# Two blocks of linear attention on one core: KV products in pairs of 64-column tiles, with a new order behind them

## The chip, the cores and the metric

The kernel runs on one core of one Trainium2 chip. The metric is the device time of one execution in microseconds (us); lower is better. The time before is the median of three runs. The profile is one execution, taken by the hardware profiler; its times count from the first instruction of the program.

The engines have these names in the profile: PE is TensorE (matrix products), PEld its weight loads, DVE is VectorE, ACT is ScalarE, POOL is GpSimd, SP is SyncE, which here only issues DMAs. A product has a stationary operand, which PEld loads, and a moving one, which streams through the array; the result lands in PSUM, and DVE or ACT bring it back into SBUF.

## The reference

Two blocks of linear attention, A and B, read the same x (2048 x 640) with weights of their own; a gate per row mixes their outputs. There are 32 heads of Dh = 20 columns.

```python
def block(x, wqkv, wo):
    q, k, v = heads(x @ wqkv)                 # 32 heads of 20
    phi = lambda t: where(t > 0, t + 1, exp(t)) + 1e-6
    pq, pk = phi(q), phi(k)
    kv = einsum("bhsd,bhse->bhde", pk, v)     # 20 x 20 for each head
    z = pk summed over s
    o = (pq @ kv) / (pq . z + 1e-6)
    return o @ wo                             # heads side by side
g = sigmoid((x * gate_w).sum(-1))
out = g * block(A_x, A_wqkv, A_wo) + (1 - g) * block(A_x, B_wqkv, B_wo)
```

## The kernel before

S = 2048 rows are 16 tiles of P = 128, D = 640 columns are DT = 5 chunks of 128, and HF = 320 is half of D. For each block b the kernel goes through these steps:

- `k_chunk` (L225, products L216) makes phi(k) of 128 rows into pk, and `q_unit` (L274, products L280) makes phi(q), turned, into pqT[b].
- `g_all` (L692) makes G = x^T phi(k), 640 x 640, in GT: two halves `lo, hi = GT` of 320 columns, with five chunks of 128 rows each. Chunk 4 comes from `g_pass` (L306); the other four come from one level of Strassen's scheme in `g_strassen` (L374, products L369), which computes seven products of sums. The sums are DVE's work. In between stands `rec_pass` (L509): the denominators, whose products den (L175) have 32 weight columns and 256 moving columns and run in four column tiles of the array; then reciprocals, a DMA through DRAM (`r_store`, `r_load`) that spreads them, and `scale` (L569), which multiplies pqT by them on DVE. `p_diff` (L543) is a DVE difference of two parts of pqT[0].
- `kv_mm` (L450, products L455) makes wv^T G, so the rows are those of v and the columns those of k. Only the 20 x 20 blocks on the diagonal are wanted. It therefore takes groups of columns of widths WB = (120, 120, 80) in each half: NW = 6 groups of six, six and four heads. For each group five products over the chunks accumulate in PSUM. `kv_mask` (L460) multiplies the groups by maskE, a pattern of ones in 20 x 20 blocks, on DVE and puts them into KVA: two operations for each half.
- `m_mm` (L483) multiplies each group of KVA by its rows of wo, two products of 320 columns. The result M = kv wo goes to DRAM (`m_store`, L489) and comes back in another layout (`m_load`, L493).
- At the end, the output pq_A M_A + pq_B M_B, with the gate in pq, is again made by Strassen's scheme: class `Pair` (L593, products in `prod`, L579) has products p1 to p7 for the two row tiles i and i + 8, five accumulating products of 320 columns each. `p1` and `p5` are copied out of PSUM by ACT. `p_sums` (L548) and `m_sum` (L559) are the sums that they need, on DVE: p5 of pair i needs p_sums(.., (1,)) of its 128 rows, and TM[0], which is m_sum(0).

The order of instructions on each engine is that of the program text around the change (`tc.manual_schedule`, L723); the preparation at the start, on POOL among others, is ordered by a scheduler.

In stage A the KV products are in `kv_a` (L470), between k_chunk(1, 1) and k_chunk(1, 2); `m_a(k)` (L498), one group at a time, stands between later chunks, from k_chunk(1, 4) on.

In stage B (L754 to L810) they stand where the output products begin. The eight PSUM banks are oz0, oz1, ox0, ox1 (for p1 and p5) and s0 to s3. The order is: KV products of the first half into s2, its mask, pairs[0].p1, a scale, KV products of the second half into s3, its mask, m_sum(0), m_b(0), pairs[1].p1, m_b(1), m_b(2), pairs[2].p1, p_sums, m_b(3), m_b(4), p_sums, pairs[3].p1, m_b(5), the two loads of M_B, pairs[0].p5, p_sums. `m_b(k)` (L767) is two products (L485), into s0 and s1 for even k and s2 and s3 for odd k, two copies, and a store; both copies of m_b(0) are ACT's, and of the others the first is ACT's and the second DVE's.

wo is loaded by `load_wo` (L665), four DMAs, so that the rows of a group lie on partitions 0 to w. In stage A this stands after the load of wv; in stage B inside g_strassen (L422).

Of the kernel before, what the change touches and what calls it, by code (L numbers as in the profile page):

```python
# [8 lines left out]
P = 128  # L9
FP32 = mybir.dt.float32  # L10
BF16 = mybir.dt.bfloat16
ACT = mybir.ActivationFunctionType
ALU = mybir.AluOpType

S, D, H = 2048, 640, 32
Dh = D // H
DT = D // P
# [4 lines left out]
HF = D // 2  # L22
TW = 4
WB = (120, 120, 80)
NW = 6
EPS = 1e-6
RB = 256
SH = S // 2
# [3 lines left out]
def kernel(  # L32
# [11 lines left out]
    nc = tc.nc  # L44
# [32 lines left out]
    wo_sb = [None, None]  # L77
    ident = persist.tile([P, P], BF16, name="ident")
    headE = persist.tile([P, H], BF16, name="headE")
    maskE = persist.tile([P, WB[0]], BF16, name="maskE")  # L80
    KVA = persist.tile([P, NW, WB[0]], BF16, name="KVA")
    R = [persist.tile([P, 4 * RB], BF16, name=f"R{h}") for h in range(2)]
    ones = persist.tile([P, H], BF16, name="ones")
# [55 lines left out]


    make_identity(nc, ident[:])
    nc.gpsimd.memset(maskE[:], 1.0)
    for sign, base in ((1, 0), (-1, Dh - 1)):
        nc.gpsimd.affine_select(
            out=maskE[:], in_=maskE[:], pattern=[[-sign * Dh, WB[0] // Dh], [0, Dh]],
            compare_op=ALU.is_ge, fill=0.0, base=base, channel_multiplier=sign,
        )
    nc.gpsimd.memset(headE[:], 1.0)
    for sign, base in ((1, 0), (-1, TW - 1)):
        nc.gpsimd.affine_select(  # L150
# [223 lines left out]
    def g_strassen(b, den):  # L374

        x11, x12 = [xn[:, k:k + hc, 0:ic] for k in (0, hc)]
        x22 = xn[:, hc:ST, ic:2 * ic]
        b11 = pk[:, 0:hc, 0:HF]
        b21, b22 = [pk[:, hc:ST, n * HF:(n + 1) * HF] for n in range(2)]
        lo, hi = GT  # L380

        def temp(name):
            return work.tile([P, 2, HF], FP32, tag="osb", name=name, bufs=3)

        def add(dst, pt, sb):
            nc.vector.tensor_tensor(out=dst, in0=pt[:, :, 0:HF], in1=sb[:], op=ALU.add)

        even, odd = ps("gs0", 0), ps("gs1", 1)
        g_prod(even, x11, b11, True, 0, 1 - b)
        rec = den()  # L390
        rec(0)
        g_prod(even, x11, b11, True, 1 - b)
        p1 = temp("p1")
        nc.scalar.copy(out=p1[:], in_=even[:, :, 0:HF])
        if b == 0:
            x_sum(3)
        else:
            rec(1)
        g_prod(odd, SX[2], TK[b][2], True)
        u2 = temp("u2")  # L400
        add(u2[:], odd, p1)
        if b == 0:
            x_sum(4)
        else:
            p_diff(part[2])
            p_diff(part[3])
        g_prod(even, x12, b21, False)
        nc.scalar.copy(out=lo[:, 0:2, :], in_=even[:, :, 0:HF])
        if b == 0:
            rec(1)  # L410
        r_load(b, 1, nc.scalar)
        if b == 0:
            wq[1] = load_w(1, "q", nc.scalar)
        scale(b, 0, 2, 0)
        g_prod(odd, SX[3], TK[b][3], False)
        u3 = temp("u3")
        add(u3[:], odd, p1)
        scale(b, 2, 4, 0)
        even = ps("gs0", 0)
        g_prod(even, SX[1], TK[b][1], True)  # L420
        if b == 1:
            load_wo(1, nc.sync)  # L422
        add(hi[:, 2:4, :], even, u3)
        scale(*((b, 0, 2, 1) if b else (b, 4, 5, 0)))
        g_prod(odd, x22, TK[b][4], False)
        if b == 1:
            scale(1, 4, 5, 0)
        add(lo[:, 2:4, :], odd, p1)
        if b == 1:
            scale(1, 2, 4, 1)  # L430
        g_prod(even, SX[4], b22, False)
        for n in range(2):
            nc.vector.tensor_tensor(out=hi[:, n, :], in0=even[:, n, 0:HF], in1=u2[:, n], op=ALU.add)
        if b == 0:
            scale(0, 0, 2, 1)
# [11 lines left out]
        )  # L447
        return zsel

    def kv_mm(b, dst, hf):  # L450

        for i, w in enumerate(WB):
            d0 = i * WB[0]
            for c in range(DT):
                nc.tensor.matmul(  # L455
                    dst[:w, d0:d0 + w], lhsT=wv[b][:, c, hf * HF + d0:hf * HF + d0 + w],
                    rhs=GT[hf][:, c, d0:d0 + w], start=(c == 0), stop=(c == DT - 1),
                )

    def kv_mask(src, hf):  # L460

        for i, n in ((0, 2), (2, 1)):
            w = WB[i]
            nc.vector.tensor_tensor(
                out=KVA[:w, 3 * hf + i:3 * hf + i + n, 0:w],
                in0=src[:w, i * WB[0]:i * WB[0] + n * w].rearrange("p (i n) -> p i n", i=n),
                in1=maskE[:w, None, 0:w].to_broadcast([w, n, w]), op=ALU.mult,
            )

    def kv_a():  # L470

        pt = ps("kvA")
        for hf in range(2):
            kv_mm(0, pt[:, hf], hf)
        for hf in range(2):
            kv_mask(pt[:, hf], hf)

    def m_rows(k):
        hf, i = divmod(k, 3)
# [2 lines left out]

    def m_mm(b, k, dst, n):  # L483
        w = m_rows(k)[1]
        nc.tensor.matmul(  # L485
            dst[:w, 0:HF], lhsT=KVA[:w, k, 0:w], rhs=wo_sb[b][:w, k, n * HF:(n + 1) * HF], start=True, stop=True,
        )

    def m_store(b, k, part):  # L489
# [174 lines left out]

    def load_wo(b, eng):  # L665
        t = wo_sb[b] = wpool.tile([P, NW, D], BF16, tag="wo", name=f"wo{'AB'[b]}")
        for hf in range(2):
            for i, n in ((0, 2), (2, 1)):
                w, d0 = WB[i], hf * HF + i * WB[0]
                eng.dma_start(  # L670
                    out=t[:w, 3 * hf + i:3 * hf + i + n, :],
                    in_=wo_dram[b][d0:d0 + n * w, :].rearrange("(j p) f -> p j f", p=w),
                )

    def q_pass(b, units, sums, lifted):

# [46 lines left out]
    with tc.manual_schedule():  # L723
# [37 lines left out]
        with late_pool("mid") as mid:  # L761
            def single(k):
                return bank(mid, f"s{k}")

            first = [single(k) for k in range(4)]

            def m_b(k):  # L767
                part = pk[:, k, :].rearrange("p (b n) -> p b n", b=2)
                w = m_rows(k)[1]
                dst = [first[n] if k == 0 else single(k % 2 * 2 + n) for n in range(2)]  # L770
                for n in range(2):
                    m_mm(1, k, dst[n], n)
                for n, copy in enumerate((nc.scalar.copy, nc.vector.tensor_copy if k else nc.scalar.copy)):
                    copy(out=part[:w, n], in_=dst[n][:w, 0:HF])
                m_store(1, k, part)

            kv_mm(1, first[2], 0)
            kv_mask(first[2], 0)
            pairs[0].p1()
            scale(1, 4, 5, 1)  # L780
            kv_mm(1, first[3], 1)
            kv_mask(first[3], 1)
            m_sum(0)
            m_b(0)
            pairs[1].p1()
            m_b(1)
            m_b(2)
            pairs[2].p1()
            p_sums(slice(0, P), (1,))
            m_b(3)  # L790
            m_b(4)
            p_sums(slice(P, 2 * P), (1,))
            pairs[3].p1()
            m_b(5)
            for h in range(2):
                m_load(1, h * P // 2, (h + 1) * P // 2)
            pairs[0].p5()
            p_sums(part[1], (1,))
        pairs[1].p5()
        for n in (2, 3):  # L800
# [74 lines left out]
```

## Time and profile before

| | us |
|---|---|
| median of 3 runs | 183.33 |
| lowest and highest run | 183.22, 184.1 |
| span of the profiled execution | 181.9 |
| PE busy | 177.9 |
| DVE busy | 147.2 |
| ACT busy | 86.3 |
| KV products, stage A (chain) | 1.49 |
| KV products, stage B (chain) | 0.74 and 0.74 |

The span goes from the first to the last instruction of the profiled execution. That execution has no time of its own in the records beside its span; the median of the runs stands 1.43 us above the span. The mean granted TensorE clock is 1.000. A row of the chain is the start, the length, and what the time went to; a row of the timeline the start, the length from first start to last end, engine, line, operation, output and inputs, shapes, count, and in brackets the idle time before it with what ended it. Matmuls overlap: one of 320 columns has a duration of 299 ns, but the next starts 136 ns after it.

### The profile page before, as it was taken

Reading aid. Unit: us, or ns where it says so; the run is one execution under the profiler, and the core shown is the slowest. Engines: PE = TensorE matmul, PEld = TensorE weight load, DVE = VectorE, ACT = ScalarE, POOL = GpSimd, SP = SyncE. Lnnn points to the kernel's source line nnn. Section 1 sums busy time; section 2 is a strip of 40 time slices with the busy share of each in tenths; the row PEclk is TensorE's granted clock in tenths of the full one; section 3 lists DMA queues with packets and bytes.
Section 4 is the critical chain, followed back from the end, with each engine's and each line's share of the span. In section 5 each row is a group of like instructions: output and inputs, shape, how many; then the busy total and the mean of one; then the engine's idle time right before and its main releaser. Section 6 shows DMA issues by size and latency. Waiting matters only on the chain.

```text
span 181.9 us, 3296 instructions
## 1 busy us (share of the span) xinstructions
PE 177.9 (98%) x1285; PEld 120.7 (66%) x1285; DVE 147.2 (81%) x248; ACT 86.3 (47%) x141; POOL 2.5 (1%) x18
## 2 busy tenths in 40 slices
PE   8999999999999999999999999999999999999993
PEld 3566657765577777877775555577778777777772
DVE  0386868989998896788778999969799999877863
ACT  2245846889961101378784779921102863111010
POOL 4100000000000000000000000000000000000000
PEclk9999999999999999999999999999999999999999
DMA  5899999423100116241115000000343570133323
GB/s 177 207 248 189 224 373 310 85 52 130 58 0 8 67 45 211 77 137 37 56 34 191 17 0 0 0 0 18 126 105 84 174 188 0 40 108 108 114 90 126
DMA packets 22598, 19.17 MB, mean 105 GB/s; under 512 B 10294, under 2 KB 21814, under 8 KB 22582
## 3 DMA queue, kind: packets, MB, share of 16 engines
q1 hardware_dynamic: 20644, 16.82, 33.4%
q10 hardware_dynamic: 1938, 2.13, 3.5%
q8 instruction: 10, 0.16, 0.4%
q14 instruction: 6, 0.05, 0.1%
HBM read 12.13 MB, written 4.53 MB: 92 GB/s over the span
## 4 chain that ended last, share of the span: by engine, by line
PE 95%; DMA 2%; ACTq 0%; DVE 0%; issue 0%
PE gs L369 17%; PE kA L216 12%; PE ox L583 12%; PE kB L216 12%; PE qB L280 12%; PE qA L280 6%; PE oz L583 6%; PE qA L290 5%; PE gB L328 2%; PE gA L328 2%; PE ow L583 2%; DMA R<-in_gate_w_dram 2%; PE qA L300 1%; PE s L485 1%; PE mA L485 1%; PE kvA L455 1%
## 5 line engine op out<-in xcount | busy, mean ns | idle before, releaser
L216 PEld LDWEIGHTS <-xT 128*128 128x128 bf16 x320 | 31.1, 98 | 12.5 <-issue 0.2
L208 DVE TENSOR_SCALAR e<-e 128x640 bf16<-128x640 bf16 (+2 forms) x53 | 18.9, 357 | 8.1 <-ACT e L203 7.4
L216 PE MATMUL kB<-wkB,xT 128*128 128x320 bf16 x160 | 23.0, 299 | 0.0
L216 PE MATMUL kA<-wkA,xT 128*128 128x320 bf16 (+1 forms) x160 | 22.6, 300 | 0.2 <-DMA wkA<-in_A_wqkv_dram 0.2
L280 PE MATMUL qB<-xT,wqB 128*128 128x512 bf16 x100 | 21.7, 379 | 0.0
L203 ACT ACTIVATE e<-kB 128x640 bf16<-128x640 f32 x16 | 11.3, 704 | 16.2 <-DMA wqB<-in_B_wqkv_dram 9.4
L280 PEld LDWEIGHTS <-wqB 128*128 128x128 bf16 x100 | 11.7, 117 | 9.7
L203 ACT ACTIVATE e<-kA 128x640 bf16<-128x640 f32 x16 | 11.2, 705 | 8.5 <-PE kA L216 8.5
L203 ACT ACTIVATE e<-qA 128x1024 bf16<-128x1024 f32 (+1 forms) x11 | 10.4, 946 | 6.4 <-PE qA L290 5.1
L633 ACT COPY u<-ox 128x320 f32<-128x320 f32 x8 | 3.4, 426 | 20.4 <-PE ox L583 20.4
L203 ACT ACTIVATE e<-qB 128x1024 bf16<-128x1024 f32 x10 | 10.2, 1024 | 5.6 <-PE qB L280 4.9
L369 PEld LDWEIGHTS <-xn 128*128 128x128 bf16 x96 | 9.2, 98 | 3.9 <-issue 0.4
L369 PEld LDWEIGHTS <-S 128*128 128x128 bf16 x96 | 9.4, 98 | 3.6
L280 PE MATMUL qA<-xT,wqA 128*128 128x512 bf16 x50 | 11.0, 379 | 0.0
L212 DVE SCALAR_TENSOR_TENSOR pk<-kB,e 128x640 bf16<-128x640 f32 x12 | 9.9, 825 | 1.3
L583 PEld LDWEIGHTS <-xT 128*128 128x128 bf16 x85 | 8.1, 98 | 2.9
L583 PEld LDWEIGHTS <-pqTB 128*128 128x128 bf16 x80 | 7.8, 98 | 3.2
L583 PEld LDWEIGHTS <-pqTA 128*128 128x128 bf16 x80 | 7.7, 98 | 2.9
L369 PE MATMUL gs<-pk,xn 128*128 128x320 bf16 x64 | 9.5, 299 | 0.0
L280 PEld LDWEIGHTS <-wqA 128*128 128x128 bf16 x50 | 5.9, 117 | 4.8
L290 PE MATMUL qA<-xT,wqA 128*128 128x512 bf16 x40 | 9.0, 379 | 0.0
L210 DVE TENSOR_TENSOR pk<-pk,e 128x640 bf16<-128x640 bf16 x12 | 5.9, 493 | 2.8 <-ACT pk L207 2.1
(122 smaller groups left out, 297.7 us busy)
## 6 DMA issues: line engine op xcount, KB each, us to landing
out_dram<-pk SPq DMA_DIRECT2D x14, 160.0 KB, 1.8
xn<-in_A_x_dram SPq DMA_DIRECT2D x3, 640.0 KB, 6.3
wkB<-in_B_wqkv_dram SPq DMA_DIRECT2D x1, 800.0 KB, 4.6
wqB<-in_B_wqkv_dram ACTq DMA_DIRECT2D x1, 800.0 KB, 5.1
wvB<-in_B_wqkv_dram SPq DMA_DIRECT2D x1, 800.0 KB
MA<-mA_dram SPq DMA_DIRECT2D x1, 800.0 KB, 4.2
MB<-mB_dram SPq DMA_DIRECT2D x2, 400.0 KB, 4.5
wqA<-in_A_wqkv_dram SPq DMA_DIRECT2D x2, 320.0 KB, 4.2
```

Source lines behind the costliest of these rows:

```text
L203: nc.scalar.activation(out=e[:], in_=src, func=ACT.Exp)
L208: nc.vector.tensor_scalar(e[:], e[:], 1.0, EPS, op0=ALU.min, op1=ALU.add)
L210: nc.vector.tensor_tensor(out=dst, in0=dst, in1=e[:], op=ALU.max)
L212: nc.vector.scalar_tensor_tensor(out=dst, in0=src, scalar=1.0 + EPS, in1=e[:], op0=ALU.add, op1=ALU.max)
L216: nc.tensor.matmul(pt[:, hf, 0:w], lhsT=xT[:, c, i * P:(i + 1) * P], rhs=wk[b][:, c, hf * HF:hf * HF + w], start=(c == 0), stop=(c == DT - 1),
L280: nc.tensor.matmul(pt[:, u, :], lhsT=mixed(wq[b][:, c, :], m), rhs=xT[:, c, n * HB:(n + 1) * HB], start=(c == 0), stop=(c == DT - 1),)
L290: nc.tensor.matmul(pt[:, u, :], lhsT=mixed(wq[b][:, c, :], m + u), rhs=xT[:, c, n * HB:(n + 1) * HB], start=(c == 0), stop=(c == DT - 1),)
L328: nc.tensor.matmul(pt[:, hf, 0:HF], lhsT=xn[:, i, c * P:(c + 1) * P], rhs=pk[:, i, hf * HF:(hf + 1) * HF], start=(i == 0), stop=(i == ST - 1),
L369: nc.tensor.matmul(pt[:, n, 0:HF], lhsT=left[:, i, n * P:(n + 1) * P], rhs=right[:, i, :], start=(first and i == 0), stop=(i == hc - 1), s ...
L485: nc.tensor.matmul(dst[:w, 0:HF], lhsT=KVA[:w, k, 0:w], rhs=wo_sb[b][:w, k, n * HF:(n + 1) * HF], start=True, stop=True,)
L583: nc.tensor.matmul(dst, lhsT=left[:, c, r0:r0 + P], rhs=right[:, c, :], start=(first and c == 0), stop=(c == DT - 1), skip_group_check=not ...
L633: nc.scalar.copy(out=self.u6[:], in_=self.at("x"))
```

## The change

- WT = 60: a group of 120 becomes two of 60 (three heads each), a group of 80 becomes 60 and 20. `kv_groups(k)` gives both, the first with its output on PSUM partitions 0 to 59, the second on 64 to 123 (or 64 to 83). `kv_mm` issues them in turn with tile_position (0, 0) and (0, 64), and the chunks in the order 4, 2, 3, 0, 1. All six groups go into one bank, 60 columns each; both halves are made in one pass.
- `kv_mask` takes four operations: the first rows of all six groups, then the second rows of two, two, and the two narrow ones. There are two masks, maskE[0] and maskE[1], the second shifted for the rows from 64 on. KVA keeps its columns, with rows 60 to 63 between the two parts; it is zeroed at the start, on POOL, as the blocks off the diagonal are no longer written.
- `m_mm` contracts over 124 rows (or 84) instead of 120 (or 80), and `load_wo` puts the rows of wo to match, with six DMAs instead of four.
- In stage B pairs[0].p1 comes ahead of the KV products, and these are in one piece; m_sum(0) moves up into `g_strassen`, behind p_diff(part[3]); pairs[1].p1 and pairs[2].p1 come between the KV products and m_b(0); m_b(0) and m_b(1), and m_b(2) and m_b(3), stand together; pairs[0].p5 comes ahead of m_b(4) and m_b(5).

```diff
--- before.py
+++ after.py
@@ -23,6 +23,7 @@
 TW = 4
 WB = (120, 120, 80)
 NW = 6
+WT = 60
 EPS = 1e-6
 RB = 256
 SH = S // 2
@@ -77,7 +78,7 @@
     wo_sb = [None, None]
     ident = persist.tile([P, P], BF16, name="ident")
     headE = persist.tile([P, H], BF16, name="headE")
-    maskE = persist.tile([P, WB[0]], BF16, name="maskE")
+    maskE = [persist.tile([P, WT], BF16, name=f"maskE{r}") for r in range(2)]
     KVA = persist.tile([P, NW, WB[0]], BF16, name="KVA")
     R = [persist.tile([P, 4 * RB], BF16, name=f"R{h}") for h in range(2)]
     ones = persist.tile([P, H], BF16, name="ones")
@@ -139,12 +140,14 @@
 
 
     make_identity(nc, ident[:])
-    nc.gpsimd.memset(maskE[:], 1.0)
-    for sign, base in ((1, 0), (-1, Dh - 1)):
-        nc.gpsimd.affine_select(
-            out=maskE[:], in_=maskE[:], pattern=[[-sign * Dh, WB[0] // Dh], [0, Dh]],
-            compare_op=ALU.is_ge, fill=0.0, base=base, channel_multiplier=sign,
-        )
+    for r in range(2):
+        nc.gpsimd.memset(maskE[r][:], 1.0)
+        for sign, base in ((1, 0), (-1, Dh - 1)):
+            nc.gpsimd.affine_select(
+                out=maskE[r][:], in_=maskE[r][:], pattern=[[-sign * Dh, WT // Dh], [0, Dh]],
+                compare_op=ALU.is_ge, fill=0.0, base=base - sign * r * P // 2, channel_multiplier=sign,
+            )
+    nc.gpsimd.memset(KVA[:], 0.0)
     nc.gpsimd.memset(headE[:], 1.0)
     for sign, base in ((1, 0), (-1, TW - 1)):
         nc.gpsimd.affine_select(
@@ -404,6 +407,7 @@
         else:
             p_diff(part[2])
             p_diff(part[3])
+            m_sum(0)
         g_prod(even, x12, b21, False)
         nc.scalar.copy(out=lo[:, 0:2, :], in_=even[:, :, 0:HF])
         if b == 0:
@@ -447,33 +451,38 @@
         )
         return zsel
 
-    def kv_mm(b, dst, hf):
-
-        for i, w in enumerate(WB):
-            d0 = i * WB[0]
-            for c in range(DT):
-                nc.tensor.matmul(
-                    dst[:w, d0:d0 + w], lhsT=wv[b][:, c, hf * HF + d0:hf * HF + d0 + w],
-                    rhs=GT[hf][:, c, d0:d0 + w], start=(c == 0), stop=(c == DT - 1),
-                )
-
-    def kv_mask(src, hf):
-
-        for i, n in ((0, 2), (2, 1)):
-            w = WB[i]
+    def kv_groups(k):
+
+        hf, i = divmod(k, 3)
+        w = WB[i]
+        return [(r * P // 2, hf, i * WB[0] + r * WT, min(WT, w - r * WT)) for r in range(2)]
+
+    def kv_mm(b, dst):
+
+        for k in range(NW):
+            for i, c in enumerate((4, 2, 3, 0, 1)):
+                for p0, hf, d0, w in kv_groups(k):
+                    nc.tensor.matmul(
+                        dst[p0:p0 + w, k * WT:k * WT + w], lhsT=wv[b][:, c, hf * HF + d0:hf * HF + d0 + w],
+                        rhs=GT[hf][:, c, d0:d0 + w], start=(i == 0), stop=(i == DT - 1), tile_position=(0, p0),
+                    )
+
+    def kv_mask(src):
+
+        src = src[:, 0:NW * WT].rearrange("p (k n) -> p k n", k=NW)
+        for r, ks, w in ((0, slice(0, NW), WT), (1, slice(0, 2), WT), (1, slice(3, 5), WT), (1, slice(2, NW, 3), WB[2] - WT)):
+            rows = slice(r * P // 2, r * P // 2 + w)
+            n = len(range(NW)[ks])
             nc.vector.tensor_tensor(
-                out=KVA[:w, 3 * hf + i:3 * hf + i + n, 0:w],
-                in0=src[:w, i * WB[0]:i * WB[0] + n * w].rearrange("p (i n) -> p i n", i=n),
-                in1=maskE[:w, None, 0:w].to_broadcast([w, n, w]), op=ALU.mult,
+                out=KVA[rows, ks, r * WT:r * WT + w], in0=src[rows, ks, 0:w],
+                in1=maskE[r][rows, None, 0:w].to_broadcast([w, n, w]), op=ALU.mult,
             )
 
     def kv_a():
 
         pt = ps("kvA")
-        for hf in range(2):
-            kv_mm(0, pt[:, hf], hf)
-        for hf in range(2):
-            kv_mask(pt[:, hf], hf)
+        kv_mm(0, pt[:, 0])
+        kv_mask(pt[:, 0])
 
     def m_rows(k):
         hf, i = divmod(k, 3)
@@ -482,8 +491,9 @@
 
     def m_mm(b, k, dst, n):
         w = m_rows(k)[1]
+        rows = P // 2 - WT + w
         nc.tensor.matmul(
-            dst[:w, 0:HF], lhsT=KVA[:w, k, 0:w], rhs=wo_sb[b][:w, k, n * HF:(n + 1) * HF], start=True, stop=True,
+            dst[:w, 0:HF], lhsT=KVA[:rows, k, 0:w], rhs=wo_sb[b][:rows, k, n * HF:(n + 1) * HF], start=True, stop=True,
         )
 
     def m_store(b, k, part):
@@ -664,13 +674,15 @@
 
     def load_wo(b, eng):
         t = wo_sb[b] = wpool.tile([P, NW, D], BF16, tag="wo", name=f"wo{'AB'[b]}")
-        for hf in range(2):
-            for i, n in ((0, 2), (2, 1)):
-                w, d0 = WB[i], hf * HF + i * WB[0]
-                eng.dma_start(
-                    out=t[:w, 3 * hf + i:3 * hf + i + n, :],
-                    in_=wo_dram[b][d0:d0 + n * w, :].rearrange("(j p) f -> p j f", p=w),
-                )
+        tv = t[:].rearrange("p (h i) f -> p h i f", h=2)
+        wide = wo_dram[b].rearrange("(h r) f -> h r f", h=2)
+        for r, n in ((0, P // 2), (1, WT)):
+            r0, p0 = r * WT, r * P // 2
+            for hf in range(2):
+                src = wide[hf, 0:2 * WB[0], :].rearrange("(j p) f -> p j f", j=2)
+                eng.dma_start(out=tv[p0:p0 + n, hf, 0:2, :], in_=src[r0:r0 + n])
+            n, d0 = (n, WB[2] - WT)[r], 2 * WB[0] + r0
+            eng.dma_start(out=tv[p0:p0 + n, :, 2, :], in_=wide[:, d0:d0 + n, :].rearrange("h p f -> p h f"))
 
     def q_pass(b, units, sums, lifted):
 
@@ -774,27 +786,24 @@
                     copy(out=part[:w, n], in_=dst[n][:w, 0:HF])
                 m_store(1, k, part)
 
-            kv_mm(1, first[2], 0)
-            kv_mask(first[2], 0)
             pairs[0].p1()
             scale(1, 4, 5, 1)
-            kv_mm(1, first[3], 1)
-            kv_mask(first[3], 1)
-            m_sum(0)
+            kv_mm(1, first[2])
+            kv_mask(first[2])
+            p_sums(slice(0, P), (1,))
+            pairs[1].p1()
+            pairs[2].p1()
             m_b(0)
-            pairs[1].p1()
             m_b(1)
+            pairs[3].p1()
             m_b(2)
-            pairs[2].p1()
-            p_sums(slice(0, P), (1,))
             m_b(3)
+            p_sums(slice(P, 2 * P), (1,))
+            pairs[0].p5()
             m_b(4)
-            p_sums(slice(P, 2 * P), (1,))
-            pairs[3].p1()
             m_b(5)
             for h in range(2):
                 m_load(1, h * P // 2, (h + 1) * P // 2)
-            pairs[0].p5()
             p_sums(part[1], (1,))
         pairs[1].p5()
         for n in (2, 3):
```

## The prediction

> **What bounds the kernel now.** I read the page first (busy times, then the shares of the chain that ended last), then the chain in order of time, then single stretches of the timeline.
>
> ```profile
> span 181.9 us, 3296 instructions
> ...
> PE 177.9 (98%) x1285; PEld 120.7 (66%) x1285; DVE 147.2 (81%) x248; ACT 86.3 (47%) x141; POOL 2.5 (1%) x18
> ...
> PE 95%; DMA 2%; ACTq 0%; DVE 0%; issue 0%
> ```
>
> The chain in order of time (start, length, what):
>
> ```profile
> 70.25 2.72 PE kB L216 x20
> 72.96 1.49 PE kvA L455 x30
> ...
> 137.76 0.74 PE s L455 x15
> 138.50 0.68 PE ox L583 x5
> 139.18 0.74 PE s L455 x15
> ...
> 145.65 0.68 PE oz L583 x5
> ```
>
> The page says that TensorE is busy for 98% of the span, and that 95% of the last chain is TensorE with nothing waited for. The pieces of the chain touch each other: 138.50 + 0.68 = 139.18, and so on. So a nanosecond taken from TensorE's queue is a nanosecond of the total, and a nanosecond in which TensorE waits is one lost, because no idle time later takes it up. The KV products that the change rewrites (L455) are 1.49 us in stage A and 0.74 + 0.74 = 1.48 us in stage B: 2.97 us of 181.9, so even a large gain here is a small part. The span is 181.9 and the median of the runs 183.33; the 1.43 us between them lie outside the span, and I leave them as they are. Everything below is a difference to the span. For this kernel a measurement can tell about 0.5%, or 0.92 us, from no change.
>
> **The products themselves.** Before, a pass has 30 products, of 120x120 and 80x80. After, it has 60 (30 pairs, of 60 columns beside 60, or 60 beside 20), each pair in two column tiles that can run side by side. The trace has no pair of this size. Nearest are the old products and the den products (L175), which run four side by side in tiles of 32 columns.
>
> ```profile
> 137.65 0.38 PE L455 MATMUL s<-GT,wvB 128*120 128x120 bf16 x4
> 138.15 0.35 PE L455 MATMUL s<-GT,wvB 128*80 128x80 bf16 x5
> L455 PE MATMUL s<-GT,wvB 128*120 128x120 bf16 x20 | 1.4, 218 | 0.0
> L455 PE MATMUL s<-GT,wvB 128*80 128x80 bf16 x10 | 0.7, 204 | 0.0
> 120.94 0.30 PE L328 MATMUL gB<-pk,xn 128*128 128x320 bf16 x1
> 121.17 0.29 PE L175 MATMUL denB<-pqTB,zsel 128*32 128x256 bf16 x4
> 121.18 0.10 PEld L175 LDWEIGHTS <-zsel 128*32 128x32 bf16 x4
> L175 PEld LDWEIGHTS <-zsel 128*32 128x32 bf16 x80 | 2.0, 96 | 0.6 <-DVE zsel L444 0.3 <-issue 0.3
> 121.17 1.27 PE L175 MATMUL denB<-pqTB,zsel 128*32 128x256 bf16 x40
> 122.37 2.35 PE L369 MATMUL gs<-pk,xn 128*128 128x320 bf16 x16
> ```
>
> The step from one start to the next: four products of 120 take 0.38 in all and one takes 0.218, so the step is (0.38 - 0.218) / 3 = 54 ns. For 80: (0.35 - 0.204) / 4 = 37 ns. The line through both is 0.43 ns a column; at 60 columns it gives 28 ns, and I take 30 for one product of 60 with its weight load.
>
> Do two such products share those 30 ns? The den rows say yes for tiles of 32: four products that last about 0.27 each are over 0.29 after the first began, so they start within 0.02, and four weight loads with a mean of 96 ns are done in 0.10 together. Ten rounds of four have starts from 121.17 to 121.17 + 1.27 - 0.28 = 122.16, so a round takes 0.11, about what 256 columns cost alone at 0.43 ns. I take 30 ns a pair. The ends: 26 ns below (a line with less overhead), 60 above (nothing shared). The forecast lies at the low end because the den rows are the nearest.
>
> Going into column tiles and out of them costs something as well. A product of 320 columns has a step of 2.72 / 20 = 0.136; gB's last starts at 120.94, so the next would start at 121.08, but den starts at 121.17: 0.09. At the other side den's last round starts at 122.16, its step of 0.11 is over at 122.27, and gs starts at 122.37: 0.10. Together 0.2 us a pass, counted in full.
>
> A pass then takes 30 x 0.030 + 0.2 = 1.10 us. Stage A: 1.10 - 1.49 = -0.39. Stage B: 1.10 - 1.48 = -0.38. **Sum -0.77 us.** Break-even for the products alone is (1.485 - 0.2) / 30 = 43 ns a pair.
>
> [...]
>
> **Masks, zeros, weights of wo.** DVE has four masks a pass as before, with 640 columns in sum as before (360 + 120 + 120 + 40 against 240 + 80, twice). I cost them at nothing in stage A, where their first reader on TensorE, mA, comes behind three k_chunks, 30 products of the 0.136 us worked out above. The POOL additions stand at the start of the kernel.
>
> ```profile
> 1.00 0.20 POOL L142 MEMSET maskE<- 128x120 bf16 x1
> 1.29 0.30 POOL masks.py:199 TENSOR_SCALAR_AFFINE_SELECT ident<-ident 128x128 bf16<-128x128 bf16 x1
> 3.62 1.25 PE L240 MATMUL xt<-ident,xn 128*128 128x128 bf16 x10
> 133.44 1.76 SPq L670 DMA_DIRECT2D woB<-in_B_wo_dram  x4
> woB<-in_B_wo_dram SPq DMA_DIRECT2D x2, 100.0 KB, 4.3
> ```
>
> The zeroing of KVA (720 columns, at most 6 x 0.20 = 1.2) goes ahead of the identity, which was ready at 1.59 and is then ready by about 2.8; TensorE reads it first at 3.62. Nothing, with 0.8 to spare. wo takes six DMAs instead of four. In B they begin at 133.44 at 0.44 each, so the last is issued at about 135.7 and lands 4.3 later, at 140.0. The products that read it (m_b) come from 140.7 on (worked out below), and SP has nothing else until then. Nothing.
>
> **m_sum(0) moved ahead.** It leaves the stretch after the KV products and goes into stage B's Strassen products.
>
> ```profile
> 140.42 0.98 DVE L539 TENSOR_TENSOR TM<-MA 128x1600 bf16<-128x1600 bf16 x1
> 130.25 1.23 DVE L572 TENSOR_TENSOR pqTB<-pqTB,R 128x2048 bf16<-128x2048 bf16 x1 [0.96 <-DMA R<-rB_dram]
> 137.80 0.89 DVE L433 TENSOR_TENSOR GT<-gs,u 128x320 bf16<-128x320 f32 x2
> ```
>
> It takes 0.98, and stands just ahead of the scale that waited 0.96 for a DMA: it fills a hole. If some 0.1 spills over, the next reader with a wait is the KV product on the last GT chunk: DVE finishes that at 137.80 + 0.89 = 138.69. After the change TensorE first does pairs[0].p1 (from 137.6, 0.68), then enters the tiles (0.09), and the late chunk is the 19th pair at the earliest (18 x 0.03): about 138.9. Nothing. pairs[0].p1 waits for the same DVE add as the old first KV product.
>
> **The new order behind the KV products in B.** I count from the start of pairs[1].p1: time 0, which is 137.60 + 0.68 (pairs[0].p1) + 0.09 + 0.90 + 0.10 = 139.37 in the span. A block of five is 0.68, an m_b (two products of 320 columns) 0.272. TensorE then has p1(1) 0, p1(2) 0.68, m_b(0) 1.36, m_b(1) 1.63, p1(3) 1.91, m_b(2) 2.59, m_b(3) 2.86, p5(0) 3.14, m_b(4) 3.82, m_b(5) 4.09, p5(1) 4.37, p1(4) 5.05, p5(2) 5.73.
>
> ```profile
> 139.95 0.55 DVE L464 TENSOR_TENSOR KVA<-s,maskE 120x240 bf16<-120x240 f32 x2 [0.21 <-PE s L455]
> 139.21 0.43 ACT L612 COPY xn<-ox 128x320 f32<-128x320 f32 x1 [9.37 <-PE ox L583]
> 141.24 0.75 ACT L774 CAST pk<-s 120x320 bf16<-120x320 f32 x2
> 141.32 0.88 DVE L774 CAST pk<-s 120x320 bf16<-120x320 f32 x2
> 143.72 0.48 DVE L774 CAST pk<-s 80x320 bf16<-80x320 f32 x1
> 144.12 2.28 DVE L539 TENSOR_TENSOR pqTA<-pqTA,pqTB 128x1280 bf16<-128x1280 bf16 x3
> 151.76 1.36 PE ow L583 x10
> 144.75 2.02 SPq L494 DMA_DIRECT2D MB<-mB_dram  x2
> MB<-mB_dram SPq DMA_DIRECT2D x2, 400.0 KB, 4.5
> ```
>
> A copy starts 0.03 after the chain piece that it reads (139.18, 139.21), so about 0.3 after its product's start. On ACT it lasts 0.43, and back to back 0.32 apart (0.75 for two); on DVE 0.48, and 0.40 apart. ACT: p1(2)'s copy from 1.56 (end of its piece 1.53, plus 0.03), then m_b(0) twice at 1.88 and 2.20, then m_b(1) at 2.52, done at 2.95. m_b(3) writes the bank that this last copy reads, and wants to start at 2.86: with a wake-up it starts at 3.0. **A stall of 0.14** that before had slack, since there p1 stood after each one or two m_b. Behind it everything shifts by 0.14.
>
> DVE: two old masks took 0.55, so four take about 1.1; they follow the last KV product, and m_b(0) comes at 1.36. No stall, 0.2 to spare. The cast of m_b(4) starts at 3.82 + 0.14 + 0.14 (its second product) + 0.33 = 4.43, that of m_b(5) at 4.83, and the p_sums of rows 256 to 511 at 5.23, done 0.81 later: 6.04. The p5(2) that reads it wants to start at 5.73 + 0.14 = 5.87: **a stall of about 0.21**. Before, these sums were done at 144.12 + 0.81 = 144.93, over 0.5 before that block (the chain has it from 145.65). The cause is that p5(0) now stands ahead of m_b(4) and m_b(5), so the casts come later while p5(2) does not. The sums for p5(1) are done near 4.35 against 4.51: no stall, but close.
>
> MB: the last cast ended at 144.20 and the second load, issued at about 146.3, landed 4.5 later, at 150.8. Now the cast ends at 139.37 + 4.83 + 0.48 = 144.7, so MB lands at 151.3, against TensorE's need near 151.6 (its first product with MB starts one product's latency ahead of the piece at 151.76). Nothing, with 0.3 to spare.
>
> **Sum.** -0.77 + 0.14 + 0.21 = -0.42 us: a span of 181.5 and a time of 183.33 - 0.42 = 182.9.
>
> **The rivals.**
> *No sharing at this size.* The place is the KV pass: each small product takes its own 30 ns. For it: the forecast needs four instructions fed every 30 ns, where den needs only eight every 110. Against: den's loads and products start together. A pass is 60 x 0.03 + 0.2 = 2.0, so +0.51 and +0.52, with the stalls +0.35: +1.4, 184.7. With both stalls it loses against before from a pair of (2.97 - 0.4 - 0.35) / 60 = 37 ns on. [...]
> *The stalls do not come.* ACT and DVE are quicker at handing over than I add up; the gain stays whole: -0.77, 182.6. For it: each stall is the difference of sums with errors of 0.1. Against: both orders of copies are fixed.
> *MB comes late.* The 0.3 to spare goes, since six stores and two loads stand in a row on SP. A last store that lands 0.7 later costs 0.4: 183.3.
>
> **How the numbers follow.** Forecast 0.58 (182.9), no sharing 0.22 (184.7; a part of it, pairs between 37 and 52 ns, ends within 0.92 of before), no stalls 0.12 (182.6), MB late 0.08 (183.3). Faster by over 0.5% means below 182.4, which needs pairs of 26 ns and no stalls (-1.0): 0.06. Slower by over 0.5%, above 184.25: nearly all of no sharing, and a little of MB: 0.20. Within: 0.74. The range goes from that low end, 182.4, to no sharing, 184.7.
>
> **What would show it.** In the profile after: the kvA piece of the chain near 1.1 (2.0 if nothing is shared); starts two by two in the KV lines, as den has them by fours; an idle TensorE ahead of m_b(3) and of p5(2), released by ACT and DVE; no idle at the start. A kvA piece above 1.5 makes the forecast wrong, as does a TensorE wait of over 0.5 us in B.

## The result, and the profile after

The changed kernel takes 188.68 us (median of 6 runs, 187.82 to 189.48) against 183.42 for the kernel before (6 runs, 183.06 to 184.1): **a ratio of 1.0287, 95% interval 1.0267 to 1.0306**. The forecast was 182.9 with a range up to 184.7, so the change is slower by 5.3 us where next to nothing was forecast.

The page of the kernel after: span and instructions, busy time of the engines, the granted clock in 40 slices, the shares of the chain that ended last.

```profile
span 187.5 us, 3425 instructions
...
PE 182.8 (97%) x1340; PEld 122.6 (65%) x1345; DVE 147.6 (79%) x248; ACT 86.2 (46%) x141; POOL 3.4 (2%) x22
...
PEclk9999999999999999999999999999997899999999
...
PE 90%; DMA 6%; DVE 1%; issue 1%; SPq 0%
```

TensorE is busy for 182.8 us, 4.9 more than before: most of the loss is not waiting but products that take longer. Two slices late in the span have a granted clock below 9 tenths, and 6% of the chain is DMA. The chain of the kernel after, in order of time:

```profile
72.58 3.13 PE kvA L465 x60
75.71 4.18 PE kB L219 x30
...
139.81 3.14 PE s L465 x60
142.94 0.94 PE ox L593 x5
143.88 1.33 PE oz L593 x5
...
151.76 5.21 DMA MB<-mB_dram
157.02 1.53 PE ow L593 x10
```

A KV pass is 3.13 us where it was 1.49; the forecast had 1.10 and named a piece above 1.5 as the sign that it is wrong. The piece behind it in stage A, 30 products of 320 columns, is 4.18, and in the chain of the kernel before it is 4.07:

```profile
74.45 4.07 PE kB L216 x30
```

Leaving the column tiles costs 0.11. In stage B blocks of five, 0.68 before, take 0.94 and 1.33.

Where in the pass is the time? The same kernel, the KV line alone, in the stretches of its groups (start and end, length, PE and PEld busy with the number of instructions that touch the stretch, clock, DMA share, GB/s):

```profile
72.50:72.82 0.32, 0.31 (x20) 0.31 (x21) 1.00 0.00 0
72.82:74.07 1.25, 1.25 (x22) 0.95 (x16) 1.00 0.00 0
74.07:74.39 0.32, 0.32 (x21) 0.31 (x21) 1.00 0.00 0
74.39:75.65 1.26, 1.26 (x22) 0.95 (x15) 1.00 0.00 0
```

The first stretch holds two groups of 120 columns, ten pairs of 60 beside 60, in 0.32 us. The second holds one group of 80, five pairs of 60 beside 20, in 1.25 us: 0.25 a pair. The trace's starts say the same more finely: in the groups of 120 the two products of a pair start 3 ns apart and the pairs 30 ns apart (72.561, 72.591, 72.621); in the groups of 80 the starts alternate at 0.144 and 0.110 (73.063, 73.207, 73.317, 73.461). TensorE counts as busy all the while. The pass is 20 x 0.030 + 10 x 0.254 = 3.14 us.

The blocks of 0.94 and 1.33 are another thing. First the kernel after, then the kernel before in the same stretch of time (busy time of PE, PEld, DVE, ACT, POOL, then the clock):

```profile
142.90:143.50 0.60, 0.60 (x6) 0.45 (x6) 0.52 (x1) 0.00 (x0) 0.00 (x0) 0.95 0.00 0
143.50:146.90 3.40, 3.40 (x15) 2.20 (x14) 1.58 (x6) 1.84 (x5) 0.00 (x0) 0.51 0.01 2
146.90:147.50 0.60, 0.60 (x6) 0.52 (x5) 0.00 (x0) 0.16 (x1) 0.00 (x0) 1.00 0.41 90
```

```profile
142.90:146.90 4.00, 4.00 (x32) 2.92 (x30) 4.00 (x8) 2.78 (x8) 0.00 (x0) 1.00 0.76 237
```

For 3.4 us TensorE is granted half its clock (0.51) and a product of 320 columns has a step of 0.267 instead of 0.136; 13 steps lose 1.7 us. The timeline of the kernel after shows four m_b products in that stretch and four of the same kind after it:

```profile
145.00 1.27 PE L495 MATMUL s<-woB,KVA 124*120 124x320 bf16 x4
...
148.37 0.71 PE L495 MATMUL s<-woB,KVA 124*120 124x320 bf16 x4
```

This happens in some runs only: of the six, three have a mean granted clock of 0.991 and 189.18 to 189.48 us, three 0.999 to 1.000 and 187.82 to 188.17, so it costs 1.3 us where it comes, and the profiled run (189.25) has it.

**The account**, from the starts of the two traces. Stage A, from the den products to the last Strassen product of stage B: 83.54 before, 85.29 after, +1.75 (1.64 of KV pieces and 0.11 of leaving the tiles). From there to pairs[0].p2: 14.14 before, 18.19 after, +4.05, which are 1.66 of KV products, 0.11 of leaving the tiles, 1.68 of half clock, and TensorE waits of 0.04 (p5 of pair 1), 0.19 (p5 of pair 2) and 0.38 (MB). The products to the end +0.01, the tail behind the last product +0.25, the start -0.38. Sum 5.68; the spans are 181.86 and 187.54.

### The profile page after: what moved, and what is told of

Its sections match the earlier page's. It is cut to its first block, busy times and chain, and to the rows that moved or that the text cites. A ratio compares the mean times of both kernels' runs of the same rounds, so it can differ in the third digit from the quotient of the medians.

```text
span 187.5 us, 3425 instructions
## 1 busy us (share of the span) xinstructions
PE 182.8 (97%) x1340; PEld 122.6 (65%) x1345; DVE 147.6 (79%) x248; ACT 86.2 (46%) x141; POOL 3.4 (2%) x22
## 4 chain that ended last, share of the span: by engine, by line
PE 90%; DMA 6%; DVE 1%; issue 1%; SPq 0%
PE gs L372 16%; PE kA L219 12%; PE kB L219 12%; PE qB L283 11%; PE ox L593 10%; PE qA L283 6%; PE qA L293 5%; PE oz L593 4%; DMA MB<-mB_dram 3%; PE gA L331 2%; PE gB L331 2%; PE ow L593 2%; DMA wkA<-in_A_wqkv_dram 2%; PE s L465 2%; PE kvA L465 2%; PE qA L303 1%
```

## The experiments

**The theory**: the time goes into the changes of width, from a product of 60 columns to one of 20 (a step of about 0.14 in the trace of the kernel after) and back (0.11), where a pair of 60 takes 0.03. Groups of 80 alternate 60, 20, 60, 20 and pay this ten times, with the change on leaving the group. With one width a pass should fall from 3.13 to about 1.1, the half clock of stage B should go with it, and the time should be 182.8 to 183.4. **The rival on the pass**: 60 short instructions can't be fed fast enough, whatever their widths. **A second question**: are the steps behind the products, the stalls that the forecast saw, and MB as priced?

**All tiles of one width.** Each group is covered by two products of 60 columns that overlap in the middle, so that the number of products stays and only the width of the small ones changes. Masks, rows of M and wo follow.

```diff
     def kv_groups(k):
...
-        return [(r * P // 2, hf, i * WB[0] + r * WT, min(WT, w - r * WT)) for r in range(2)]
+        return [(r * P // 2, hf, i * WB[0] + r * (w - WT), WT) for r in range(2)]
```

> The narrow product of the two groups of 80 is made 60 columns wide (it computes columns 20 to 79 and keeps the last 20), so all 60 products of a pass are of one width; their number, the order and everything else is that of the changed kernel. [...] Rival (the feed of 120 short instructions runs dry from the 22nd product on): the number of instructions is the same, a pass stays at about 3.1 and the time at 188 to 189.

Measured: 183.65 us, 1.0013 of the kernel before (1.0003 to 1.0023). Its chain:

```profile
72.45 1.02 PE kvA L465 x60
...
137.56 1.02 PE s L465 x60
...
145.86 5.38 DMA MB<-mB_dram
```

The same 60 products, ten of them three times as wide, take 1.02 us instead of 3.13. Feeding is not the limit; the rival falls. With 0.11 for leaving the tiles the pass is 1.13, 0.36 to 0.37 under the old 1.49, and stage A's stretch shrinks by that: 83.54 to 83.17. Yet the kernel is not faster than before, and lies above the 182.8 to 183.4 that were expected. Its timeline shows why:

```profile
141.10 0.87 PE L495 MATMUL s<-woB,KVA 124*80 124x320 bf16 x4
...
142.49 0.71 PE L495 MATMUL s<-woB,KVA 124*120 124x320 bf16 x4
...
143.72 0.84 PE L593 MATMUL ox<-MA,pqTA 128*128 128x320 bf16 x5
144.64 0.85 PE L593 MATMUL oz<-TM,pqTA 128*128 128x320 bf16 x5
...
151.29 1.40 PE L593 MATMUL ow<-MB,pqTB 128*128 128x320 bf16 x9 [0.36 <-DMA MB<-mB_dram]
```

Four m_b products take 0.87 in the first row and 0.71 in the second: the 0.16 is m_b(3) waiting for its bank (it starts at 141.54; ACT's copy of m_b(1) out of that bank ends at 141.49). The last block of 0.84 before p5(2) begins at 143.72, and p5(2) at 144.64 instead of 143.72 + 0.68 = 144.40: 0.24. The first product with MB starts 0.52 later than the steps before it would have it (0.36 of that as idle PE). Together 0.93 in stage B, against 0.37 gained there: its stretch grows from 14.14 to 14.71.

**The same products in another order.** In the groups of 80 the five of 60 columns go first, then the five of 20, so each such group has two changes of width, one inside and one on leaving it, instead of ten.

```diff
-            for i, c in enumerate((4, 2, 3, 0, 1)):
-                for p0, hf, d0, w in kv_groups(k):
+            steps = [(i, c, g) for i, c in enumerate((4, 2, 3, 0, 1)) for g in kv_groups(k)]
+            if k % 3 == 2:
+                steps.sort(key=lambda s: s[2][0])
+            for i, c, (p0, hf, d0, w) in steps:
```

> The 20-wide products stay, but in the groups of 80 the five products of 60 come first and the five of 20 behind them, so there are 3 changes of width inside a pass instead of 20. Theory of the changes: a pass of 0.6 for the four groups of pairs, 0.55 for 20 single products, 0.2 for entering and leaving and 3 x 0.12 for the changes, 1.7 us; the time 183.4 + 0.4 + 0.2 to 0.7 = 184.0 to 184.5 us. Rival (a product of 20 columns is slow by itself, 0.14 us each wherever it stands): 10 x 0.14 more than the pairs alone, a pass of 2.4 to 2.6 us, and 185.5 to 187.

Measured: 185.01 us, 1.0081 (1.0068 to 1.0095). Chain:

```profile
73.01 1.55 PE kvA L467 x60
...
138.65 1.55 PE s L467 x60
```

No instruction is added or taken away, and the pass falls from 3.13 to 1.55. In the trace the 20-column products start 25 ns apart among themselves and the 60-column ones of a single tile 30; the steps over the two changes of a group are 0.12 and 0.10. The time is above the 184.0 to 184.5 that were expected: the sum allowed 0.2 to 0.7 for waits in stage B, and they are 1.00 (0.16, 0.24 and 0.60 for MB), with 0.25 more behind the last product.

**Another width of the narrow one.** Groups of 80 as 60 beside 40, which leaves the products unequal. If any change of width costs the time, the pass stays near 3.1 us and the time near 188; if only a change as large as the one from 60 to 20 does, they are 1.02 and 183.65.

```diff
-        return [(r * P // 2, hf, i * WB[0] + r * WT, min(WT, w - r * WT)) for r in range(2)]
+        n = min(WT, w // 2)
+        return [(0, hf, i * WB[0], WT), (P // 2, hf, i * WB[0] + w - n, n)]
```

> As e1_wide, but the narrow product is 40 columns wide instead of 60 (it computes columns 40 to 79 of the group and keeps the last 20); order as in the changed kernel. [...]

Measured: 183.91 us against 183.56 in that series, 1.0015 (0.9996 to 1.0034). Chain (the trace has all 60 products of a pass; where two run side by side the chain can hold one of them alone):

```profile
73.04 1.01 PE kvA L466 x54
...
138.14 1.01 PE s L466 x56
```

Unequal products cost nothing, 60 beside 40 runs like 60 beside 60 (1.01 and 1.02 in the chains). So it is not inequality: of the two widths tried beside 60, 20 costs time and 40 does not. Weight columns and moving columns were narrowed together, so the runs do not tell which of the two counts.

**Narrow in one stage only**, the other as in the first experiment (masks and wo follow):

```diff
-    def kv_groups(k):
+    def kv_groups(b, k):
...
+        if b == 0:
+            return [(r * P // 2, hf, i * WB[0] + r * WT, min(WT, w - r * WT)) for r in range(2)]
```

and the same with `b == 1`.

> The narrow products of 20 columns in stage A alone; stage B has one width of 60; order as changed. Theory of the width changes: stage A's pass 3.1 us, 2.0 more than in e1_wide, so 185.7 us. The halved clock: if a pass with 20 width changes is what brings it, it comes behind stage A's pass in some of the runs (mean clock 0.991, 1.3 us more) and never in stage B; if it belongs to stage B's order or its waits, the clock stays 1.0 here.

> The narrow products of 20 columns in stage B alone; stage A has one width of 60; order as changed. Theory of the width changes: stage B's pass 3.1 us, 2.0 more than in e1_wide, 185.7 us at a full clock, and about 187 where the clock is halved behind the pass. If the clock belongs to stage A's slow pass: no run here with 0.991.

Measured: 186.1 us for A (1.0164, 1.0133 to 1.0195), 185.84 for B (1.0137, 1.0116 to 1.0158). Chains, A then B:

```profile
73.02 3.13 PE kvA L467 x60
...
140.24 1.02 PE s L467 x60
```

```profile
73.27 1.02 PE kvA L467 x60
...
138.38 3.13 PE s L467 x60
```

The slow pass comes where the 20s are and costs 2.2 to 2.5 us over the first experiment (the median of A holds two runs with the half clock), 3.13 - 1.02 = 2.11 of it seen in the chain. On the half clock: narrow in A has it in two of six runs (0.991 and 0.989 at 187.13 and 187.63, the others 0.999 or 1.000 at 185.81 to 186.26), narrow in B in none of four. None of the other kernels' runs, about 170 with those of before, has less than 0.997. So it goes with a slow pass, also in stage A; it doesn't follow each one.

**The order alone**: the old products, with the new order behind them; the first line added is the one in g_strassen.

```diff
+            m_sum(0)
...
-            kv_mm(1, first[2], 0)
-            kv_mask(first[2], 0)
             pairs[0].p1()
             scale(1, 4, 5, 1)
-            kv_mm(1, first[3], 1)
-            kv_mask(first[3], 1)
-            m_sum(0)
+            for hf in range(2):
+                kv_mm(1, first[2 + hf], hf)
+            for hf in range(2):
+                kv_mask(first[2 + hf], hf)
...
```

> The kernel before with nothing but the new order of stage B and the earlier m_sum(0); KV products, masks and wo as before. If the stalls worked out ahead are right (m_b(3) 0.14, pairs[2].p5 0.21, and MB landing late by up to 0.4): 183.4 + 0.4 to 0.8 = 183.8 to 184.2 us. Rival (the order costs nothing by itself; the stalls in the changed kernel come from its slow KV pass): 183.4 us, within 0.1.

Measured: 183.76 us, 1.0009 (0.9987 to 1.0031). Timeline:

```profile
142.19 0.87 PE L486 MATMUL s<-woB,KVA 80*80 80x320 bf16 x4
...
144.81 0.84 PE L584 MATMUL ox<-MA,pqTA 128*128 128x320 bf16 x5
145.72 0.85 PE L584 MATMUL oz<-TM,pqTA 128*128 128x320 bf16 x5
```

The same two waits, 0.16 and 0.24 (145.72 - 144.81 - 0.68 = 0.23), and 0.12 for MB, with the old products: they belong to the order. The stretch is 0.53 longer by the trace; the runs' interval does not exclude no change.

**The products alone**: pairs of 60 with the old order (two passes of three groups in B, m_b and p1 interleaved as before); against the first experiment's kernel:

```diff
+            kv_mm(1, first[2], range(3))
+            kv_mask(first[2], range(3))
             pairs[0].p1()
             scale(1, 4, 5, 1)
-            kv_mm(1, first[2])
-            kv_mask(first[2])
-            p_sums(slice(0, P), (1,))
-            pairs[1].p1()
-            pairs[2].p1()
+            kv_mm(1, first[3], range(3, 6))
+            kv_mask(first[3], range(3, 6))
+            m_sum(0)
             m_b(0)
+            pairs[1].p1()
...
```

> The widened products of 60 (as in the run with one width) in the order of stage B of the kernel before: half a pass, mask, pairs[0].p1, half a pass, mask, m_sum(0), m_b(0) and so on. Stage A gains 0.39, stage B 0.38 less 0.2 for entering and leaving the column tiles a second time: 183.4 - 0.6 = 182.8 us. If the gain of the pairs is real but hidden somewhere else: 183.4. If the order was needed for the gain (masks late): 183.4 or more.

Measured: 184.04 us, 1.0031 (1.0019 to 1.0043): a miss, slower instead of faster. The timeline, and the chain, which names the fourth DMA of wo:

```profile
138.60 0.64 PE L464 MATMUL s<-GT,wvB 128*60 128x60 bf16 x30
139.85 0.45 PE L496 MATMUL s<-woB,KVA 124*120 124x320 bf16 x2 [0.61 <-DMA woB<-in_B_wo_dram]
```

```profile
135.00 4.71 DMA woB<-in_B_wo_dram
```

m_b(0) waits for a wo load that was issued at 135.00 and landed at 139.71. The loads follow each other at 0.65 to 0.69 (133.00, 133.69, 134.35, 135.00, 135.65) where the old four took 0.44 each; with the old order m_b(0) comes earlier and meets them. MB costs 0.24 more. The new order hides the new wo loads; neither half of the change pays by itself.

**The stalls removed.** In the first experiment's kernel, the second copy of every m_b on DVE, p_sums in smaller parts and earlier, the first MB load issued by ACT; then the same with both loads on SP (`nc.sync` twice in the last loop).

```diff
-                for n, copy in enumerate((nc.scalar.copy, nc.vector.tensor_copy if k else nc.scalar.copy)):
+                for n, copy in enumerate((nc.scalar.copy, nc.vector.tensor_copy)):
...
+            p_sums(slice(P, 2 * P), (1,))
             pairs[3].p1()
...
-            p_sums(slice(P, 2 * P), (1,))
+            p_sums(slice(2 * P, 3 * P), (1,))
...
-            for h in range(2):
-                m_load(1, h * P // 2, (h + 1) * P // 2)
-            p_sums(part[1], (1,))
+            for h, eng in enumerate((nc.scalar, nc.sync)):
+                m_load(1, h * P // 2, (h + 1) * P // 2, eng)
+            p_sums(slice(3 * P, 4 * P), (1,))
```

> One width of 60 as in e1_wide, and the three stalls of stage B taken away by order: the second copy of m_b(0) goes to DVE and p_sums of rows 128 to 255 up behind m_b(1) (ACT is free for m_b(1)'s copy earlier, so m_b(3) doesn't wait); p_sums of rows 256 to 383 alone ahead of the casts of m_b(4) and m_b(5) (so pairs[2].p5 doesn't wait); the first load of MB on ACT's queue instead of SP's, where it stood behind the last store (so the second doesn't share its time). Theory (e1_wide lost 0.16 + 0.24 + 0.52 = 0.93 us to these three, and gained 0.73 in the products): 183.4 - 0.7 = 182.6 to 182.9 us, TensorE without idle in stage B. Rival (the wait for MB is set by the stores' landing and the load's own time, and ending the first two only makes it longer): MB's stall grows to 0.9 and the time stays at 183.6.

> As e5_fixed, but both loads of MB on SP's queue as in the changed kernel. If the two loads share their time (5.4 us for the second, against 4.5 where they are issued 1.5 us apart): the stall ahead of p2 is 0.7 to 0.9 us, though the two stalls ahead of it are gone, and the time 183.4 to 183.6. If the queue doesn't matter: as e5_fixed, 182.8.

Measured: 183.47 us, 1.0000 (0.9988 to 1.0012), and 183.56 us, 1.0011 (0.9999 to 1.0022). Timeline of the first, then of the second:

```profile
145.00 0.84 PE L593 MATMUL oz<-TM,pqTA 128*128 128x320 bf16 x5
145.92 0.84 PE L593 MATMUL ox<-MA,pqTA 128*128 128x320 bf16 x5
```

```profile
151.19 1.53 PE L593 MATMUL ow<-MB,pqTB 128*128 128x320 bf16 x10 [0.34 <-DMA MB<-mB_dram]
```

Both waits of 0.16 and 0.24 are gone in both. With the load on ACT a new one of 0.24 stands in the first rows (145.92 - 145.00 - 0.68), since ACT's copies stand behind the load that it issues (0.50 us on its queue, from 144.9 on); MB still costs 0.28. With both loads on SP nothing is left but MB, and MB costs 0.50, where 0.7 to 0.9 was expected. Its load in the chain:

```profile
146.18 4.96 DMA MB<-mB_dram
```

So the wait for MB did not grow when the two others went: counted from the first KV product of stage B, the load lands after 13.32 us (151.14 - 137.82), in the first experiment after 13.75 (151.24 - 137.49). Stage B's stretch falls from 14.71 to 14.28 and 14.27, which is 0.14 and 0.13 over before. With 0.37 gained in stage A and 0.25 lost behind the last product both traces come out level with before, and so do the runs; the 182.6 to 182.9 expected of the first is missed.

**m_b earlier.** To bring MB forward, m_b(0) stands behind one p1 instead of two, p1 and m_b alternate as in the kernel before, the mask is in five parts, the p_sums of rows 256 to 511 are in one piece again, and the wo loads are in the order of need. Against the kernel with both loads on SP:

```diff
-            kv_mm(1, first[2])
-            kv_mask(first[2])
-            p_sums(slice(0, P), (1,))
+            kv_mm(1, first[3])
+            kv_mask(first[3])
             pairs[1].p1()
-            pairs[2].p1()
             m_b(0)
...
+            p_sums(slice(0, P), (1,))
+            pairs[2].p1()
...
```

> One width of 60, and stage B ordered so that M_B is stored half a microsecond earlier: pairs[1].p1, m_b(0), m_b(1), pairs[2].p1, m_b(2), m_b(3), pairs[3].p1, m_b(4), m_b(5), pairs[0].p5; the mask in five operations, those of m_b(0) and m_b(1) first; one copy on ACT and one on DVE for every m_b; the six loads of wo in the order in which m_b reads them. If the wait for MB is all that still eats the gain of the products (0.5 us in e8_sploads): no idle of TensorE in stage B and 183.4 - 0.7 = 182.7 us, at most 183.1. If MB's landing doesn't follow the last store: a stall of 0.5 stays, 183.5.

Measured: 184.29 us against 183.56, 1.0045 (1.0012 to 1.0078): a miss. DVE and PE:

```profile
140.29 1.42 DVE L476 TENSOR_TENSOR KVA<-s,maskE 60x180 bf16<-60x180 f32 x5 [0.21 <-PE s L465]
```

```profile
141.76 0.35 PE L495 MATMUL s<-woB,KVA 124*120 124x320 bf16 x1 [0.17 <-DVE KVA L476]
```

The masks take 1.42 us in a row; m_b(0) and m_b(1) wait 0.11 and 0.33 for them, and MB is still 0.44 late.

**Pairs in stage A only**, all 60 wide, stage B left as it was before (its own buffer for KVA of B, masks of its own).

```diff
+        dst = ps("kvA")[:, 0]
+        for k in range(NW):
+            hf, i = divmod(k, 3)
+            for n, c in enumerate((4, 2, 3, 0, 1)):
+                for p0, d0 in ((0, i * WB[0]), (P // 2, i * WB[0] + WB[i] - WT)):
...
```

> Pairs of one width of 60 in stage A alone, with its own masks, its own KVA and its own layout of wo; stage B wholly as in the kernel before (products, order, wo in four DMAs). If the pairs gain 0.37 us a pass and everything that gave it back lies in stage B's order and DMAs: 183.4 - 0.4 = 183.0 us, TensorE's idle as in the kernel before. If zeroing KVA and the extra masks on POOL hold up the start: the first products of k begin later and the time is 183.4 or more.

Measured: 183.2 us against 183.34, 0.9987 (0.9973 to 1.0001); 183.0 was expected. Page and chain:

```profile
span 181.5 us, 3367 instructions
```

```profile
72.81 1.02 PE kvA L488 x60
...
137.25 0.74 PE s L466 x15
...
138.66 0.74 PE s L466 x15
```

Stage A's stretch is 0.37 shorter, stage B's the old 14.14, the tail 0.16 longer. The median lies below that of both kernels, but the interval reaches 1: what is left of the idea is at most a few tenths of a microsecond.

## Why the prediction was wrong, by its own steps

**The step that failed** is "I take 30 ns a pair" applied to "30 pairs, of 60 columns beside 60, or 60 beside 20". For 20 of the 30 pairs it was right to the nanosecond: 60 beside 60 starts every 30 ns. The ten pairs of 60 beside 20 take 254 ns each. That is 10 x 0.224 = 2.2 us a pass; by the chains it is 3.13 - 1.02 = 2.11, so 4.2 in both, of the 5.8 between the forecast of 182.9 and 188.68. The forecast had priced a change of width twice a pass, "into column tiles and out of them", and sized it rightly (0.2; measured 0.093 and 0.11), but did not ask whether it happens within the pass. Its bounds, 26 to 60 ns, came from rows in which all tiles have one width, so they didn't hold the case.

The traces put it down to the changes between 60 and 20: 3.13 us with 19 changes inside a pass, 1.55 with three, 1.02 with none. What happens in TensorE at such a change is not shown.

**The second cause was not in the forecast at all**: the half clock, 1.3 us in half of the runs.

**The pair itself.** Sharing was right, and the rival "no sharing" was not what happened, though its price (2.0 a pass) lay nearest. The 20-column products of a single tile start 25 ns apart in the run that groups them, two products of 60 in different tiles 3 ns apart, as the den rows, with four starts within 0.02, had said.

**The stalls** were right in place and size: m_b(3) 0.14 forecast, 0.16 measured in each trace at full clock that has this order of m_b and its copies; p5(2) 0.21 forecast, 0.24 measured in the same. In the profiled kernel after, the half clock gives ACT and DVE time, and the first is gone, the second 0.19. The rival "the stalls do not come" falls.

**MB, "nothing, with 0.3 to spare", was wrong**: the wait is 0.38 in the kernel after and 0.52 at full clock with the quick pass. The rival that MB comes late (0.4) had the effect and about the size, but not the cause. It has the last store land later; the second load is issued 2.03 behind the end of the last cast in the kernel after and 2.01 in the first experiment, against 2.10 before. The mis-sized term is the landing of the second load. The forecast took 4.5 us from the row of before, where SP's two issues are spread over 2.02. In the kernels with pairs in stage B they follow each other more closely, and not by the new order alone: with the old order and pairs they start 1.12 apart, before 1.55. SP's timeline, after and then the first experiment:

```profile
150.80 1.44 SPq L504 DMA_DIRECT2D MB<-mB_dram  x2
```

```profile
144.92 1.41 SPq L504 DMA_DIRECT2D MB<-mB_dram  x2
```

Their second loads land 5.21 and 5.38 after issue (the chains above). In the nine traces with pairs in stage B where SP issues both, starts 0.94 to 1.12 apart go with 4.96 to 5.67; with the order alone, 1.47 apart, it is 4.9, before, 1.55 apart, 4.45, and with pairs in stage A only, 1.95 apart, 4.29. With the first load on ACT, 1.97 apart, it is 4.71. That two loads of 400 KB share the time is the author's estimate from these figures; no run varied the spacing alone.

**wo in six DMAs, "0.44 each, nothing"**: the first four issues are 0.65 apart and the fifth 1.3 long, so that the last begins 4.0 after the first instead of 2.3. In the order of the change nothing waits for them, as forecast; with the old order 0.6.

**Masks, zeroing, m_sum(0)** cost nothing that any trace shows at their places: the identity is ready at 2.18 and first read at 3.76, and no KV product waits for DVE in stage B.

**The sum.** With the failed step mended (the first experiment) the time is 183.65, inside the range but 0.75 above the 182.9. By its trace: products -0.74 (forecast -0.77), stalls +0.40 (+0.35), MB +0.52 (0), the tail behind the last product +0.25 (0), together +0.43; its runs lie 0.24 above before.

## What to carry to other kernels

When small products are packed into column tiles, look at the width of every one of them: here 60 beside 20 took 254 ns a pair and 60 beside 60 only 30, and widening the narrow products by overlap (a pass of 1.02 us) was cheaper than the changes (3.13, or 1.55 with the narrow ones grouped). A price taken from rows of one kind of work holds only for a sequence of that kind, so write the sequence of instructions out before multiplying. And where the gain is a few tenths of a microsecond ahead of a DMA on the path, ask when that DMA lands: here the load of MB, forecast at nothing, took back 0.52 of the 0.74 that the products gained in the first experiment.

## What the runs showed of the hardware

- The step over a change between a product of 60 columns and one of 20 is 0.10 to 0.14 us, where without the change it is 0.025 to 0.030, and TensorE counts as busy; 60 beside 40 costs nothing (a pass of 1.01 us, against 1.02 with one width), and two products of 60 in different column tiles start 3 ns apart and share 30 ns.
- In the profiled run of the kernel after TensorE's granted clock is 0.50 from 143.44 to 146.85, 3.41 us, and 1.00 on both sides. The fall comes 0.49 behind the end of stage B's pass of 3.14 us (139.81 + 3.14 = 142.95); behind the pass of 3.13 us in stage A of the same run the clock stays 1.00 (75.7 to 82.0). By the mean clock of a run (0.989 or 0.991, against 0.997 to 1.000) it falls in 3 of 6 runs with two such passes, 2 of 6 with one in stage A, and 0 of 4 with one in stage B. Why it falls, and why in some runs only, is not shown: one trace has it, and no run was made to move the pass in time.
- The stretch from the start of the last product to the end is 3.05 us before, 3.04 with the order alone, 3.29 or 3.30 in all kernels with pairs in both stages, and 3.21 with pairs in A alone. The last store is no slower: SP issues it 0.62 behind that start, and the wait for it ends 1.61 to 1.63 later, before, in the first experiment and with pairs in A alone. What differs is the place of this wait among SP's last five: it is the fifth before, the second with pairs in A alone and the first in the first experiment, and each wait behind it adds 0.06. Why that order changes is not shown.
